# A small early read of w_in, one warm product fewer, and another order of the first layernorm tiles in a TensorE-bound kernel

## The chip, the cores and the metric

The kernel runs on one core of one Trainium2 chip. The metric is the device time of one execution in microseconds (us). Each kernel of a comparison is executed several times, in rounds that alternate with the kernel before on the same chip. A profile is a recording of one such execution; its span, from the first to the last instruction, is about 2.2 us shorter than the time.

## The reference, cut to what matters

x has 2048 rows of 640 numbers. The output is x plus two branches over xn = layernorm(x): a state-space branch and a gated MLP.

```python
xn = _layernorm(x, axis=-1)
return x + _A_ref(xn, ...) + _B_ref(xn, B_w_in, B_w_sp, B_b_sp, B_w_out)

def _B_ref(x, w_in, w_sp, b_sp, w_out):          # w_in: 640 x 1728
    z = _gelu(jnp.einsum('bsd,df->bsf', x, w_in))
    z1 = z[..., :Fh].copy()
    z2 = _layernorm(z[..., Fh:], axis=-1)
    g = jnp.einsum('ts,bsf->btf', w_sp, z2) + b_sp[None, :, None]   # 2048 x 2048
    return jnp.einsum('bsf,fd->bsd', z1 * g, w_out)
```

`_A_ref` (cut) is a complex diagonal recurrence over 2048 steps, with a dense product ahead of it and one behind it.

## The kernel before

The kernel records every operation with what it reads and writes, and then orders them itself: TensorE in program order, every other engine by priority. Constants such as `DMA_BW0` only steer this ordering; they change no hardware setting.

```python
class _Graph:
    EPS0 = 0.12
    DMA_BW = 280e3
    DMA_BW0, DMA_T0 = 225e3, 9.0
    ...
    # next operation of an engine: of those ready within EPS0, the one with the longest work behind it
    s0 = min(max(f, o.rdy) for o in lst)
    cand = max((o for o in lst if max(f, o.rdy) <= s0 + (self.EPS0 if s0 < self.TEPS else eps)), key=lambda o: o.tail)
```

x is worked on in 16 tiles of 128 rows, numbered from 0. In the head of the kernel, loads come from SyncE's queue in the order tile 0, 1, 2, two pieces of w_in, tile 3, a piece, tile 4, a piece, tile 5. TensorE first runs eight products of zeros ("warm").

```python
FIRST = "x0 x1 x2 h002 h025 x3 h103 x4 h135 x5"        # h..: pieces of w_in
...
NW = 8
for n in range(NW):
    pe(lambda e: e.matmul(ps[:, 7, :], zero_m.ap(128), zero_m.ap(512), start=True, stop=True), ..., 0.43, "warm")
```

Tiles 0 to 2 are handled early: only centred (`xc`, VectorE), transposed by TensorE (`T`), copied out of PSUM (`xnT`), multiplied with w_in in halves, and scaled by 1/std later, inside the GELU. The means of tiles 0 and 1 come from ScalarE (`lnmean`), the mean of tile 2 from statistics on VectorE (`bn2a`, `bn2b`, `bna2`). Tiles 3 and 6 get their sums from ScalarE (`lnsum`, `lnsq`, 0.72 us each) and then pass VectorE (`lnv`), GpSimd (`rstd`) and VectorE again (`xn`). Tile 4 gets statistics on VectorE (`bn4a`, `bn4b`). Its transposed copy `xnT4` is ScalarE's.

```python
dve(lambda e: e.tensor_scalar(xc.ap(D), xm.ap(D), mean, None, op0=ALU.subtract), [xm.iv(), mi], [xc.iv(0, 1280)], ..., "xc%d" % i)

def early_bn(i):
    x, xm = xs[i].ap(D), xs[i]
    held = [xc_m[2].iv()] if i == 1 else xnT_iv(2, 3) if i == 3 else []     # "held": also wait for these
    dve(lambda e: e.bn_stats(stv[:, i, 0:6], x[:, 0:320]), [xm.iv()] + held, [siv(i, 0, 6)], 0.41, "bn%da" % i)
    ...
pe(tr, [xn.iv(0, 1280), ident_m.iv()], [bank(b)] + ..., 0.3, "T%d" % i)
...
elif i in (1, 4, 6):
    act(lambda e: e.copy(xnTv[:, :, i * 128:(i + 1) * 128], v), [bank(b)], xnT_iv(i, i + 1), ca(D, psum=True), "xnT%d" % i)
```

The "first full tile" below is the first product of tile 4, the first that runs over all 864 columns in one go. From there on TensorE finds its work ready.

Much later, in the stage of w_sp ("spatial", a Strassen-like scheme of seven products for each of eight blocks), the gated results go through two buffers in turn, and a buffer is free again only when its store has landed:

```python
gm = g_m[ng[0] % 2]
...
dve(... e.tensor_tensor(gm.ap(FH), c.ap(FH), zm.ap(...), ALU.mult), ..., "gate%d%d" % (j, h))
...
dma("sp", g_d[n], gm.ap(896), [gm.iv()], [("gd", n, n + 1)], 128 * 1792, "gst%d%d" % (j, h), sem="gst%d" % gsem)
```

## Time and profile before

| | before |
|---|---|
| time, median of three runs | 262.68 us (262.36 to 262.86) |
| the profiled execution | 263.17 us, span 261.0 us |
| first full tile's products begin | 15.62 us |
| spatial stage begins / out stage begins / last product ends | 110.68 / 192.63 / 258.39 us |

First, lines of the profile's page: the span, the busy times of the engines (PE is TensorE, PEld its weight loads, DVE VectorE, ACT ScalarE, POOL GpSimd), and the shares of the chain of waits that ended last.

```profile
span 261.0 us, 4323 instructions
...
PE 256.0 (98%) x1501; PEld 152.0 (58%) x1501; DVE 243.9 (93%) x565; ACT 179.8 (69%) x323; POOL 26.9 (10%) x50
...
PE 95%; DMA 2%; ACT 1%; SPq 0%; issue 0%; DVE 0%
```

TensorE is busy 98% of the span and is 95% of the chain. So time can be won only where TensorE waits. The view of who waited for whom lists those places (engine, line, what it waited for: us in total, times, longest us):

```profile
PE ps L490 <- DVE arena L477: 1.2, 1, 1.2
PE ps L649 <- ACT arena L620: 0.7, 1, 0.7
PE ps L611 <- DVE arena L536: 0.3, 1, 0.3
PE ps L670 <- DMA arena<-in_B_w_in_dram: 0.2, 1, 0.2
```

All four lie in the head. The timeline of the head shows them in order (start, us, engine, line, operation, tiles, count, and in brackets the idle time just before with what ended it):

```profile
4.57 0.74 PE L611 MATMUL ps<-arena 128*128 128x128 bf16 x5
...
4.78 0.49 DVE L542 BATCH_NORM_STATS2 arena<-arena 128x6 f32<-128x320 bf16 x1 [0.43 <-DMA arena<-in_A_x_dram]
5.20 0.37 DVE L536 TENSOR_SCALAR arena<-arena 128x640 bf16<-128x640 bf16 x1
...
5.62 0.45 PE L611 MATMUL ps<-arena 128*128 128x128 bf16 x5 [0.31 <-DVE arena L536]
...
6.32 1.07 PE L670 MATMUL ps<-arena 128*128 128x432 bf16 x4 [0.25 <-DMA arena<-in_B_w_in_dram]
...
7.51 4.18 PE L670 MATMUL ps<-arena 128*128 128x432 bf16 x22
...
9.78 0.22 DVE L577 SCALAR_TENSOR_TENSOR arena<-arena 128x1 f32<-128x1 f32 x1 [1.46 <-ACT arena L575]
...
11.53 0.44 PE L611 MATMUL ps<-arena 128*128 128x128 bf16 x5
...
11.73 0.62 ACT L680 ACTIVATE arena<-ps,arena 128x432 bf16<-128x432 f32 x1 [0.78 <-PE ps L670]
...
12.34 0.72 ACT L573 ACTIVATE arena<-arena 128x640 bf16<-128x640 bf16 x1
...
13.61 0.44 PE L611 MATMUL ps<-arena 128*128 128x128 bf16 x5
...
13.66 0.73 ACT L575 ACTIVATE arena<-arena 128x640 bf16<-128x640 bf16 x1
...
14.88 0.69 ACT L620 COPY arena<-ps 128x640 bf16<-128x640 bf16 x1
...
15.62 0.91 PE L649 MATMUL ps<-arena 128*128 128x432 bf16 x4 [0.66 <-ACT arena L620]
```

Tile 1's centring (5.20) ran behind the statistics of tile 2 (4.78), which waited for tile 2's load, and tile 1's transposes (5.62) waited for it. And ScalarE idled 0.78 us before 11.73, then did the two sums of tile 6 (12.34 and 13.66) between GELUs, and so started the copy of tile 4 only at 14.88, 0.83 us after the transposes that it copies had ended (13.61 plus 0.44). TensorE waited 0.66 us for that copy.

### The profile page before, as it was taken

The page shows a single profiled execution, that of the slowest core. Times are in us where ns is not written, and L with a number is a line of the kernel's source. Part 1 is how long each engine was busy: PE and PEld are TensorE (multiplying, and loading weights), DVE is VectorE, ACT ScalarE, POOL GpSimd, SP SyncE. Part 2 cuts the span into 40 slices and gives each one's busy share as a digit, 9 for nine tenths or more (in the row PEclk, how much of TensorE's full clock was granted, in tenths as well). Part 3 has the DMA queues.
Part 4 walks back from the last instruction along what each step waited for, and adds up shares of the span by engine and source line. Part 5 has one row for each costly group of instructions (what it writes and reads, how often), then busy time and mean ns, then how long its engine had stood idle before and what let it go on. Part 6 is the DMA issues. An engine that isn't in the chain of part 4 may idle for free.

```text
span 261.0 us, 4323 instructions
## 1 busy us (share of the span) xinstructions
PE 256.0 (98%) x1501; PEld 152.0 (58%) x1501; DVE 243.9 (93%) x565; ACT 179.8 (69%) x323; POOL 26.9 (10%) x50
## 2 busy tenths in 40 slices
PE   7989999999999999999999999999999999999996
PEld 3555554444446777755555555555566677777774
DVE  5799999699999999999999999999999999999943
ACT  6799999989986445442333496865979897893110
POOL 3557265500000000000000000000000000000000
PEclk9999999999999999999999999999999999999999
DMA  6955689998505873399999966992133555545621
GB/s 188 332 107 103 136 176 211 241 301 219 81 0 125 166 201 136 104 313 192 230 222 187 244 156 136 232 242 69 54 113 95 139 146 121 148 134 157 171 104 53
DMA packets 89603, 42.31 MB, mean 162 GB/s; under 512 B 72334, under 2 KB 89582, under 8 KB 89582
## 3 DMA queue, kind: packets, MB, share of 16 engines
q1 hardware_dynamic: 89294, 41.93, 66.1%
q8 instruction: 12, 0.20, 0.3%
q10 hardware_dynamic: 288, 0.11, 0.2%
q14 instruction: 9, 0.07, 0.1%
HBM read 12.27 MB, written 12.45 MB: 95 GB/s over the span
## 4 chain that ended last, share of the span: by engine, by line
PE 95%; DMA 2%; ACT 1%; SPq 0%; issue 0%; DVE 0%
PE ps L1063 31%; PE ps L1211 23%; PE ps L649 20%; PE ps L743 17%; PE ps L670 2%; PE ps L1218 2%; DMA arena<-in_B_w_in_dram 2%; ACT arena L680 1%; SPq L373 0%; PE ps L611 0%; ACT arena L575 0%; ACT arena L573 0%; ACT arena L620 0%; DVE arena L1276 0%; PE ps L860 0%
## 5 line engine op out<-in xcount | busy, mean ns | idle before, releaser
L1063 PE MATMUL ps<-arena 128*128 128x432 bf16 x448 | 82.1, 346 | 0.0
L1063 PEld LDWEIGHTS ps<-arena 128*128 128x128 bf16 x448 | 43.6, 98 | 38.3 <-ACT arena L1076 0.9
L1211 PE MATMUL ps<-arena 128*128 128x320 bf16 (+2 forms) x456 | 64.7, 296 | 0.0
L1211 PEld LDWEIGHTS ps<-arena 128*128 128x128 bf16 x456 | 44.0, 98 | 17.3 <-ACT ps L1240 0.3
L649 PE MATMUL ps<-arena 128*128 128x432 bf16 x280 | 51.8, 346 | 0.7 <-ACT arena L620 0.7
L849 ACT ACTIVATE arena<-arena 128x512 bf16<-128x512 bf16 x70 | 46.3, 712 | 8.5 <-DVE arena L853 8.1
L649 PEld LDWEIGHTS ps<-arena 128*128 128x128 bf16 x280 | 34.6, 124 | 17.0 <-ACT arena L620 1.1
L743 PE MATMUL ps<-arena 128*128 128x512 bf16 x200 | 43.3, 379 | 0.0
L1076 ACT ACTIVATE arena<-ps,arena 128x432 f32<-128x432 f32 (+1 forms) x32 | 19.6, 617 | 22.7 <-PE ps L1063 22.7
L743 PEld LDWEIGHTS ps<-arena 128*128 128x128 bf16 x200 | 19.6, 98 | 23.5
L772 DVE SCALAR_TENSOR_TENSOR arena<-arena 128x512 f32<-128x512 bf16 x35 | 25.5, 742 | 0.0
L748 ACT CAST arena<-ps 128x512 bf16<-128x512 f32 x40 | 22.2, 600 | 3.6 <-PE ps L743 3.5
L853 DVE TENSOR_TENSOR arena<-arena 128x1024 bf16<-128x1024 bf16 (+1 forms) x42 | 23.9, 592 | 0.0
L727 ACT ACTIVATE arena<-ps 128x864 bf16<-128x864 f32 x16 | 14.2, 891 | 14.1 <-PE ps L649 11.6
L1232 DVE TENSOR_TENSOR arena<-ps,arena 128x320 bf16<-128x320 f32 (+1 forms) x40 | 18.6, 480 | 5.2 <-PE ps L1218 3.9
L1018 DVE TENSOR_TENSOR arena<-arena 128x1024 bf16<-128x1024 bf16 x32 | 21.0, 682 | 0.8 <-DMA arena<-in_B_w_sp_dram 0.8
L1240 ACT COPY ps<-ps 128x320 f32<-128x320 f32 x24 | 9.9, 413 | 16.5 <-PE ps L1211 16.3
L794 DVE TENSOR_TENSOR arena<-arena 128x512 f32<-128x512 f32 (+2 forms) x40 | 21.2, 548 | 0.0
L777 DVE SCALAR_TENSOR_TENSOR arena<-arena 128x256 bf16<-128x256 bf16 (+1 forms) x35 | 16.5, 475 | 0.0
L774 DVE SCALAR_TENSOR_TENSOR arena<-arena 128x256 bf16<-128x256 bf16 (+1 forms) x35 | 16.5, 473 | 0.0
L1178 DVE TENSOR_TENSOR arena<-arena 128x640 bf16<-128x640 bf16 x32 | 15.2, 479 | 0.0
L663 ACT ACTIVATE arena<-arena 128x864 bf16<-128x864 bf16 x12 | 11.2, 930 | 0.0
(116 smaller groups left out, 256.7 us busy)
## 6 DMA issues: line engine op xcount, KB each, us to landing
g_scratch<-arena SPq DMA_DIRECT2D x16, 224.0 KB, 2.8
z_scratch<-arena SPq DMA_DIRECT2D x16, 216.0 KB, 1.9
arena<-z_scratch SPq DMA_DIRECT2D x8, 432.0 KB, 4.4
arena<-in_A_x_dram SPq DMA_DIRECT2D x16, 160.0 KB, 3.3
base_scratch<-arena SPq DMA_DIRECT2D x16, 160.0 KB, 2.3
arena<-base_scratch SPq DMA_DIRECT2D x16, 160.0 KB, 2.3
out_dram<-arena SPq DMA_DIRECT2D x15, 160.0 KB, 2.3
arena<-in_B_w_in_dram SPq DMA_DIRECT2D x7, 216.0 KB, 4.4
```

What stands on the lines that cost most here:

```text
L649: r = e.matmul(ps[:, b + h, 0:FG], lhs(k), winv[:, k, hcol * FH + h * FG:hcol * FH + (h + 1) * FG], start=(k == 0), stop=(k == ND - 1))
L743: r = e.matmul(ps[:, b, :], btv[:, ri, k, q * 128:(q + 1) * 128], xnTv[:, k, tq * 512:(tq + 1) * 512], start=(k == 0), stop=(k == ND - 1))
L748: act(lambda e: e.copy(o[:, ri, tq], ps[:, b, :].rearrange("p (m j) -> p j m", j=8)), [bank(b)], [l_m.iv((q * 8 + j) * 1024 + ri * 512 + t ...
L772: dve(lambda e: e.scalar_tensor_tensor(tv, prev, lr, cur, op0=ALU.mult, op1=ALU.add), pr + [l_iv(q, j)] + cr, [t.iv()], cd(512) + PTR, nm ...
L794: tt = lambda o, a, b, op: (lambda e: e.tensor_tensor(o, a, b, op))
L849: act(lambda e, pv=pv, hv=hv, lo=lo, sc=sc: e.activation(pv, hv[:, lo:lo + 2, 1:257], ACT.Identity, scale=sc), [h.iv(), Civ(cn)], [m.iv((q ...
L853: dve(lambda e, mv=mv, lq=lq: e.tensor_tensor(lq, lq, mv, ALU.add), li + [m.iv(0, 1024 * n)], li, cd(512 * n, 2), "fix%s%d%d" % (nm, q0, j))
L1018: dve(lambda e: e.tensor_tensor(o.ap(1024), x.ap(1024), y.ap(1024), op), [x.iv(), y.iv()], [o.iv()], cd(1024, 2), "%s_%d" % (name, j))
L1063: r = e.matmul(ps[:, bk, 0:FG], lv_[:, k, :], rv[k], start=(first and k == 0), stop=(k == 7), skip_group_check=True)
L1076: act(lambda e: e.activation(o, pb(bk), ACT.Identity, bias=bias), [bank(bk)] + bi, [dst], ca(FG, psum=True, ptr=1), name)
L1211: r = e.matmul(ps[:, bk, c0:c1], lf(q), rf(q)[:, c0:c1], start=(first and q == 0), stop=(q == 7), skip_group_check=True)
L1232: dve(lambda e: e.tensor_tensor(o[0][:, c0:c1], ps[:, bk, c0:c1], y[0][:, c0:c1], ALU.add), [bank(bk), y[1]], [o[1]], cd(c1 - c0), "%s_%d" ...
```

## The change

The intent: let a tiny read (sixteen rows of w_in, 4 KB) make the first contact with w_in early from ScalarE's queue ("touch"); start the first transposes earlier by dropping a warm product; centre tile 1 before tile 2's statistics; and give the ordering model other figures, so that ScalarE and VectorE take their work in another order.

```diff
     DMA_BW = 280e3
+    DMA_BW1, DMA_T1 = 320e3, 14.0
     DMA_BW_T = 215e3
-    DMA_BW0, DMA_T0 = 225e3, 9.0
+    DMA_BW0, DMA_T0 = 205e3, 4.6
 ...
-                    dma_free = at + op.nbytes / (self.DMA_BW0 if at < self.DMA_T0 else self.DMA_BW)
+                    dma_free = at + op.nbytes / (self.DMA_BW0 if at < self.DMA_T0 else self.DMA_BW1 if at < self.DMA_T1 else self.DMA_BW)
 ...
+        dma("act", dk_m.ap(128)[0:16, :], B_w_in[0:640:40, FH:FH + 128], [], [dk_m.iv()], 4096, "touch", bias=9500)
 ...
-        NW = 8
+        NW = 7
 ...
-            held = [xc_m[2].iv()] if i == 1 else xnT_iv(2, 3) if i == 3 else []
+            held = [xc_m[2].iv()] if i == 1 else [xc_m[1].iv(0, 1280)] if i == 2 else xnT_iv(2, 3) if i == 3 else []
 ...
-            pe(tr, [...], [...], 0.3, "T%d" % i)
+            pe(tr, [...], [...], 0.5 if i == 0 else 0.3, "T%d" % i)
```

What it does to the built order of the head (g0.1 is the GELU of half 1 of tile 0). SyncE's order is unchanged.

```
ScalarE before: g0.0 lnsq3 g1.0 g2.0 g0.1 lnsum6 g2.1 lnsq6 g3.0 xnT4 g3.1 g1.1
ScalarE after:  g0.0 lnsq3 g2.0 g1.0 lnsum6 lnsq6 g0.1 g2.1 g1.1 xnT4 g3.0 g3.1
VectorE before: bna0 bn2a xc1 bn2b xnT0b bna2 xc2 bn1a bn1b xnT2 bna1 lnv3 bn4a bn4b bna4 xn3 ...
VectorE after:  bna0 xc1 bn2a bn2b xnT0b bna2 xc2 bn1a xnT2 bn1b bna1 bn4a bn4b lnv3 bna4 bn5a bn5b xn3 ...
```

More of the change, by code (lines that the diff above doesn't have):

```diff
@@ L612, in tr @@
                 return r
-            pe(tr, [xn.iv(0, 1280), ident_m.iv()], [bank(b)] + ([bank(6)] if i == 0 else []), 0.3, "T%d" % i)
+            pe(tr, [xn.iv(0, 1280), ident_m.iv()], [bank(b)] + ([bank(6)] if i == 0 else []), 0.5 if i == 0 else 0.3, "T%d" % i)
             if i == 0:
```

## The prediction

Its "third transposes" are those of tile 3, its "fifth tile" is tile 4.

> **What bounds the kernel now.** TensorE. The page has PE busy 98% of a 261.0 us span, and the chain of waits is 95% PE. From 18.2 us on, the timeline shows its products back to back. The view of who waited for whom gives PE four waits: 1.2 us at the start, 0.3 us for the centred second tile (VectorE), 0.2 us for the first w_in piece (DMA), 0.7 us for ScalarE's copy of the transposed fifth tile. So only the head, up to the first full tile's products at 15.62 us, can change and its gain should reach the end, since later work moves along with it.
>
> **What the change does, by timeline and build order**. PE: one warm product fewer. ScalarE: one DMA issue first; the two sums over tile 6 now stand ahead of the last three half-tile GELUs, where they stood among them. VectorE: second tile centred before the third's statistics; fifth tile's statistics ahead of a wait on ScalarE. SyncE: unchanged.
>
> **Costs.**
> 1. Warm product: the first transposes were ready at 4.24 us (centring ends) but queued behind the eighth warm product (4.15, spaced 0.43 us) and began at 4.57. With seven they begin at about 4.3: -0.28 us.
> 2. Centring of tile 1: its mean is there at 4.54, but VectorE waited for the third tile (landed 4.76) and did its statistics first, centring at 5.20. Now about 4.56: -0.64. Its transposes' copy ends near 6.45 instead of 6.81.
> 3. Touch: the first w_in piece landed at 6.28, but 15 of its 16 parts were in by 5.45; one packet took 1.3 us. If first contact with w_in is the cause, the touch hides it: piece 1 at 5.5 to 5.9, later loads 0 to 0.4 us earlier. The Trainium skill (DMA: Bandwidth & Descriptors, Issuing engines are not separate DMA queues) says both queues share the same 16 engines; no run here shows that yet. On ScalarE the issue costs about 0.45 us (SyncE's issue spacing), table load 1.28 us, then a 0.2 us activation: done near 2.7, before tile 0 lands at 2.96. Free.
> 4. Together the 22-product block starts near 7.15 instead of 7.51. Without faster loads this is lost again at the third transposes (11.53), which hang on tile 3's landing (7.58) through ScalarE and GpSimd.
> 5. ScalarE idled 10.95 to 11.73, then did two tile sums (0.72 each), so the fifth tile's copy came at 14.88 although its transposes were done at 14.07. Now the first sum fills that hole: copy at about 14.03, done 14.7. PE's 0.66 us stall before 15.62 nearly vanishes: first full tile near 14.75 (14.4 with faster loads).
>
> **Predicted.** 0.85 us (loads unchanged) to 1.2 us off; taken as 1.0 off. 261.7 us, 8 in 10 between 261.1 and 262.4; faster by over 2% 0.005, within 2% 0.985, slower 0.01.
>
> **What would show it.** First transposes at 4.3; second copy ending 6.45; first w_in product before 6.0; tile 4's copy near 14.0; first full tile at 14.4 to 14.8; later stages unchanged.
>
> **What would make it wrong.** The touch's slow first reads delaying tile 0 itself (it gates the whole head); the slow packets being random, not first contact; ScalarE late for tile 0; the PE clock rising later: warm products run every 0.43 us against 0.216 later, and the Trainium skill (TensorE: Matmul & The Clock Gate, The HAM clock gate) says a free-running window of about 3.4 us decides that, so it may differ from run to run.

## The result, and the profile after

| | before | after |
|---|---|---|
| median of six runs, same chip | 262.72 us (262.17 to 262.86) | 262.49 us (261.87 to 263.36) |
| mean of six runs | 262.61 | 262.51 |
| ratio, with 95% interval | | 0.9996 (0.9976 to 1.0017) |
| span of the profiled execution | 261.0 | 260.6 |
| first full tile | 15.62 | 14.95 (-0.67) |
| spatial stage begins | 110.68 | 110.00 (-0.68) |
| out stage begins | 192.63 | 192.14 (-0.49) |
| last product ends | 258.39 | 257.90 (-0.49) |

A ratio is the mean time of one kernel's fast runs over that of the other's of the same rounds, so it is not quite the ratio of the medians, or of the means of all runs. The time is the same within the interval: 0.1 us off in the mean, where 1.0 was predicted, and the median lies 0.1 us above the top of the predicted range. The interval reaches from about 0.6 us faster to 0.4 us slower, so this measurement alone rules out 1.0 but not a gain of half a microsecond.

The page, as before (span, TensorE, chain):

```profile
span 260.6 us, 4320 instructions
...
PE 256.2 (98%) x1496; PEld 152.0 (58%) x1500; DVE 244.3 (94%) x565; ACT 180.2 (69%) x323; POOL 26.4 (10%) x50
...
PE 92%; DMA 3%; DVE 1%; SPq 1%; issue 1%; ACT 0%; POOL 0%
```

TensorE's waits:

```profile
PE ps L494 <- DVE arena L481: 1.2, 1, 1.2
PE ps L1067 <- ACT arena L1080: 0.2, 1, 0.2
```

Three of the four waits are gone from the list, as intended. A new one of 0.2 us has come up in the spatial stage (L1067 is its products, L1080 its evictions on ScalarE). It is 0.36 us of idle TensorE at 180.4 when the neighbouring products are counted, and it is where the lead of 0.68 us becomes 0.49.

The timeline of the head, to be set against the one of before:

```profile
4.39 1.43 PE L615 MATMUL ps<-arena 128*128 128x128 bf16 x10
...
4.67 0.39 DVE L540 TENSOR_SCALAR arena<-arena 128x640 bf16<-128x640 bf16 x1 [0.21 <-ACT arena L535]
...
5.77 1.52 PE L674 MATMUL ps<-arena 128*128 128x432 bf16 x4
...
7.41 4.18 PE L674 MATMUL ps<-arena 128*128 128x432 bf16 x22
...
9.19 0.49 DVE L587 BATCH_NORM_STATS2 arena<-arena 128x6 f32<-128x320 bf16 x1 [0.44 <-DMA arena<-in_A_x_dram]
...
9.99 0.20 DVE L581 SCALAR_TENSOR_TENSOR arena<-arena 128x1 f32<-128x1 f32 x1
...
10.82 0.73 ACT L577 ACTIVATE arena<-arena 128x640 bf16<-128x640 bf16 x1
...
11.68 0.74 ACT L579 ACTIVATE arena<-arena 128x640 bf16<-128x640 bf16 x1
...
11.69 0.45 PE L615 MATMUL ps<-arena 128*128 128x128 bf16 x5
...
13.66 0.44 PE L615 MATMUL ps<-arena 128*128 128x128 bf16 x5
...
14.20 0.69 ACT L624 COPY arena<-ps 128x640 bf16<-128x640 bf16 x1
...
14.95 0.90 PE L653 MATMUL ps<-arena 128*128 128x432 bf16 x4
```

Tile 1 is centred at 4.67 and its transposes follow tile 0's without a gap (ten in one row at 4.39). The first w_in product runs at 5.77 instead of 6.32; the trace has the first piece of w_in landing at 5.50 instead of 6.28. The block of 22 products, however, starts only 0.10 us earlier (7.41), because the four products ahead of it, which began early, ran at the slow clock: 1.52 us where they had taken 1.07. Tile 3's transposes begin at 11.69, later than before, although tile 3 landed earlier (7.09 against 7.58). VectorE took tile 4's statistics first (9.19, which waited 0.44 us for tile 4's load), and `lnv3`, whose inputs were ready at 9.6, came behind them at 9.99; in before it ran at 9.78, ahead of tile 4's statistics. Then the part that worked: the two sums of tile 6 now stand at 10.82 and 11.68, the first in ScalarE's old hole, and the copy of tile 4 starts at 14.20, 0.10 us after its transposes ended (they began at 13.66).

So in these two profiles the whole gain of the head is the order on ScalarE. That leaves four questions. Is it the ScalarE order in general? Is the touch worth anything? Is what was gained in the head given back in the spatial stage? And why do the times show less than the profiles?

### The profile page after: what moved, and what is told of

Same layout as the page of the kernel before. It is cut to its first block, busy times and chain, and to the rows that moved or that the text cites. A ratio compares the mean times of both kernels' runs of the same rounds, so it can differ in the third digit from the quotient of the medians.

```text
span 260.6 us, 4320 instructions
## 1 busy us (share of the span) xinstructions
PE 256.2 (98%) x1496; PEld 152.0 (58%) x1500; DVE 244.3 (94%) x565; ACT 180.2 (69%) x323; POOL 26.4 (10%) x50
## 4 chain that ended last, share of the span: by engine, by line
PE 92%; DMA 3%; DVE 1%; SPq 1%; issue 1%; ACT 0%; POOL 0%
PE ps L1067 29%; PE ps L1215 23%; PE ps L653 20%; PE ps L747 16%; DMA arena<-in_A_x_dram 2%; PE ps L1222 2%; DMA arena<-in_B_w_sp_dram 1%; SPq L374 1%; PE ps L674 1%; PE ps L615 0%; DVE arena L1022 0%; ACT arena L853 0%; DVE arena L857 0%; POOL arena L594 0%; ACT arena L1080 0%
## 5 line engine op out<-in xcount | busy, mean ns | idle before, releaser
L1067 PE MATMUL ps<-arena 128*128 128x432 bf16 x448 | 82.1, 346 | 0.2 <-ACT arena L1080 0.2
L1067 PEld LDWEIGHTS ps<-arena 128*128 128x128 bf16 x448 | 43.7, 98 | 38.4 <-ACT arena L1080 0.9
L1080 ACT ACTIVATE arena<-ps,arena 128x432 f32<-128x432 f32 (+1 forms) x32 | 19.7, 617 | 22.8 <-PE ps L1067 22.8
L747 PEld LDWEIGHTS ps<-arena 128*128 128x128 bf16 x200 | 19.6, 98 | 23.5
L731 ACT ACTIVATE arena<-ps 128x864 bf16<-128x864 f32 x16 | 14.2, 891 | 14.0 <-PE ps L653 11.1
L667 ACT ACTIVATE arena<-arena 128x864 bf16<-128x864 bf16 x12 | 11.1, 928 | 0.0
```

The costliest lines, as they stand in the source:

```text
L747: r = e.matmul(ps[:, b, :], btv[:, ri, k, q * 128:(q + 1) * 128], xnTv[:, k, tq * 512:(tq + 1) * 512], start=(k == 0), stop=(k == ND - 1))
L1067: r = e.matmul(ps[:, bk, 0:FG], lv_[:, k, :], rv[k], start=(first and k == 0), stop=(k == 7), skip_group_check=True)
L1080: act(lambda e: e.activation(o, pb(bk), ACT.Identity, bias=bias), [bank(bk)] + bi, [dst], ca(FG, psum=True, ptr=1), name)
```

## The experiments

In most experiments the order of each engine is written out as a list and enforced, since otherwise every edit would move other instructions as well. "Gap" below is the time from tile 3's transposes to the first full tile, the stretch that ScalarE's order decides. Each profile is one execution; where a statement rests on several, it says on how many. All outputs were correct. Each experiment is compared with eleven runs of the kernel before on the same chip.

### First call: one part of the change alone, or all but one

**act_only**: the kernel before with ScalarE's order of the change, nothing else.

```diff
-  g0.0 lnsq3 g1.0 g2.0 g0.1 lnsum6 g2.1 lnsq6 g3.0 xnT4 g3.1 g1.1
+  g0.0 lnsq3 g2.0 g1.0 lnsum6 lnsq6 g0.1 g2.1 g1.1 xnT4 g3.0 g3.1
```

> The kernel before with one thing changed: ScalarE's order of the changed kernel (both sums over tile 6 ahead of the last three half-tile GELUs of tiles 0 to 2, the fifth tile's copy ahead of tile 3's GELUs). No touch, eight warm products, VectorE order of before. Theory A (the order on ScalarE is all of the gain in the head; touch, warm product and centring give nothing that lasts): first full tile's products at 14.9 to 15.0 us instead of 15.62, third transposes still near 11.5, time 0.4 to 0.7 us below the kernel before. Theory B (the touch and the earlier centring carry the gain): full tile no earlier than 15.3, time within 0.3 us of before.

Measured: ratio 0.9982 (0.9959 to 1.0006), median 262.75 against 263.41 us. Its timeline:

```profile
12.08 0.45 PE L642 MATMUL ps<-arena 128*128 128x128 bf16 x5
...
14.80 0.69 ACT L651 COPY arena<-ps 128x640 bf16<-128x640 bf16 x1
...
15.55 0.91 PE L680 MATMUL ps<-arena 128*128 128x432 bf16 x4
```

The copy of tile 4 starts at 14.80, 0.17 us after its transposes ended, and the gap is 3.47 us where the kernel before had 4.09. The profiled head as a whole was not ahead of the first profile of before (15.55 against 15.62), because tile 3 landed late in this execution (8.16), which put its transposes at 12.08. The same execution waited 0.6 us for the transposing load of tile 8 near 22.6 us. What follows: the order on ScalarE alone takes 0.6 us off the gap. The start of the tile and the time, which theory A put at 14.9 to 15.0 us and 0.4 to 0.7 us below before, are less clear: 15.55, and 0.40 us in the mean.

**touch_only**: the kernel before with the touch, nothing else.

```diff
+        dma("act", dk_m.ap(128)[0:16, :], B_w_in[0:640:40, FH:FH + 128], [], [dk_m.iv()], 4096, "touch", bias=9500)
```

> The kernel before plus the touch alone. Theory A (slow DMA packets are scattered, not a first contact with w_in): about 20 packets of w_in over 150 ns as in both traces so far, first piece of w_in landing anywhere from 5.4 to 6.3, time within 0.2 us of before. Theory B (first contact): first piece at 5.5 or earlier, no w_in packet over 500 ns, and the loads behind it earlier; even so at most 0.2 us faster, since ScalarE still holds the full tile at 15.6.

Measured: ratio 1.0008 (0.9986 to 1.0029), median 263.68. The first piece of w_in landed at 5.64, tile 3 at 7.10, and tile 2 at 5.07, later than before's 4.76. In its timeline tile 1's transposes then wait for tile 2's statistics, just as the order of before makes them:

```profile
5.09 0.49 DVE L575 BATCH_NORM_STATS2 arena<-arena 128x6 f32<-128x320 bf16 x1 [0.66 <-DMA arena<-in_A_x_dram]
...
5.93 0.71 PE L644 MATMUL ps<-arena 128*128 128x128 bf16 x5 [0.62 <-DVE arena L569]
```

Tile 3's transposes came at 12.10, the full tile at 16.19, the gap was 4.09 again. The touch alone gives no time.

**no_touch**: the change without the touch (its other orders kept).

```diff
-        dma("act", dk_m.ap(128)[0:16, :], B_w_in[0:640:40, FH:FH + 128], [], [dk_m.iv()], 4096, "touch", bias=9500)
```

> The changed kernel without the touch, every order as in the changed kernel. Theory A: the same as the changed kernel within 0.2 us (mean near 262.5), full tile near 14.9. Theory B: 0.4 us or more slower than the changed kernel, first w_in piece landing near 6.2 again. A third possibility, that the touch itself costs: tile 0 lands at 2.96 instead of 3.06 and this is 0.1 us faster.

Measured: ratio 0.996 (0.9938 to 0.9982), median 262.42. The full tile was at 14.91, with w_in landing at 6.03. So the head of the change is had without the touch.

**after_fixed**: the change itself, orders written out: a repetition on this chip.

> The changed kernel again, built with its orders written out (same instructions), as a repeat and a check of the writing-out. Expected as the changed kernel: 262.1 to 262.7 median, ratio 0.998 to 1.000, full tile at 14.8 to 15.2, third transposes at 11.5 to 11.8. If the changed kernel's 0.67 us in the head is real in every run, the ratio over five rounds should be near 0.9975; if it is lost again in the spatial stage, the start of that stage is 0.6 us early and the last product less than 0.3 us early.

Measured: ratio 0.9971 (0.9948 to 0.9994), median 262.72, full tile 15.22. Here the change is 0.69 us faster in the mean (262.65 against 263.34). In the first measurement it was 0.10. The change's own level hardly moved (262.51 there, 262.65 here); that of the kernel before did (262.61 there, 263.34 here).

The spans say the same more clearly. Mean span of the runs: before 261.16, act_only 260.78, touch_only 261.43, no_touch 260.20, after_fixed 260.22.

No_touch and after_fixed both waited in the spatial stage near 168 us. In no_touch the waits of VectorE and of TensorE there, from the view of who waited for whom:

```profile
DVE arena L1135 <- DMA g_scratch<-arena: 1.0, 1, 1.0
```

```profile
PE ps L1094 <- ACT arena L1107: 0.6, 1, 0.6
```

and the timeline of that stretch:

```profile
164.62 0.61 DVE L1135 TENSOR_TENSOR arena<-arena 128x864 bf16<-128x864 bf16 x1 [1.03 <-DMA g_scratch<-arena]
...
165.74 1.34 ACT L880 ACTIVATE arena<-arena 128x512 bf16<-128x512 bf16 x2 [1.03 <-DVE arena L845]
...
166.98 0.60 ACT L1107 ACTIVATE arena<-ps,arena 128x432 f32<-128x432 f32 x1
...
167.63 1.27 PE L1094 MATMUL ps<-arena 128*128 128x432 bf16 x6 [0.56 <-ACT arena L1107]
```

This is a chain. A gate product on VectorE (L1135) waits 1.03 us for a store out of the buffer that it is to write; the trace has that store issued at 159.51 and landed at 164.60, 5.1 us later, where the median of such stores is 2.8. (In before it took 4.5 us, 160.23 to 164.71.) VectorE's next results (L845) come late, so ScalarE's rotation (L880) waits 1.03 us, so the eviction of a spatial product (L1107) starts only at 166.98, so TensorE waits 0.56 us for the bank. The theory now had a rival to test: that a faster head only arrives earlier at this wait and gives its lead back there.

### Second call: take the wait for the store away

**after_g3**, **before_g3**: the change and the kernel before with a third gate buffer. **best_g3**: the third buffer, no touch, and `lnv3` ahead of tile 4's statistics, `xnT4` ahead of g1.1.

```diff
+        g_m.append(Mem(st_m.lo, 1792))           # space that is free by then
-                gm = g_m[ng[0] % 2]
+                gm = g_m[ng[0] % 3]
-            gsem = n % 2
+            gsem = n % 3
```

> The changed kernel with a third buffer for the gated tile (the statistics' memory, free by then), so that gate product 40 on VectorE need not wait for the store of gate 30. Theory A (the head's gain is taken back near 167.7 us, where TensorE waits for ScalarE, which waits for VectorE, which waits for that store): no TensorE wait over 0.1 us near 167 to 169, from the spatial stage's first product to the last product of all 147.7 to 148.0 us instead of 148.2 to 148.65, time 0.3 to 0.5 us below the changed kernel, ratio to before 0.995 to 0.9965. Theory D (VectorE is late there by its own work, or any transfer in that congested stretch would do): a wait of 0.3 us or more stays within 160 to 185 us and the interval stays above 148.2.

> The kernel before with the third gate buffer, nothing else. Theory A: TensorE waited only 0.12 us there in the profile of before, so at most 0.2 us faster than before (ratio 0.999 to 1.000), interval from first spatial product to the last 147.8 to 148.0. If the store also held the kernel before in most of its runs, up to 0.4 us faster.

> Changed kernel without the touch, third gate buffer, and two moves in the order: on VectorE tile 3's variance step ahead of tile 4's statistics (so that it doesn't wait for tile 4's landing), on ScalarE the fifth tile's copy ahead of tile 1's second GELU. Theory A (the VectorE order of the change holds the third transposes behind tile 4's landing): third transposes at 11.1 to 11.3 instead of 11.55 to 11.76, first full tile at 14.4 to 14.6 instead of 14.9 to 15.2, time 0.7 to 1.0 us below the changed kernel, ratio to before 0.992 to 0.9945. If tile 4's landing isn't what holds it: third transposes stay at 11.5 or later and the gain is the buffer's alone.

Measured: after_g3 1.0014 (0.9994 to 1.0035), before_g3 1.0035 (1.0011 to 1.0059), best_g3 1.0042 (1.0014 to 1.007). All three are above 1, and the wait was still there. Best_g3 missed in the head as well. With `lnv3` ahead of tile 4's statistics tile 3's transposes were expected at 11.1 to 11.3 and came at 11.72, because `xn3` still stood behind tile 5's statistics (11.22). In best_g3:

```profile
DVE arena L1185 <- DMA g_scratch<-arena: 2.3, 1, 2.3
```

```profile
PE ps L1144 <- ACT arena L1157: 1.7, 1, 1.7
```

The edit was wrong. It hands out buffers in program order, but VectorE runs the gates of the later blocks in swapped pairs (gate 41 before gate 40), so the third buffer moved the wait for the same store to a gate that runs even earlier. The runs that were to remove the wait made it longer. They still serve, as the far end of a scale (VectorE's wait for the store, and TensorE's wait behind it, in the same profile; from the same view for every profile):

| VectorE waited | TensorE waited | in |
|---|---|---|
| 2.3 | 1.7 | best_g3 |
| 1.5 | 0.9 | before_g3 |
| 0.9 to 1.0 | 0.2 to 0.7 | act_only, no_touch, after_fixed, dve_only2, after_g3, and from the fifth call warm_only |
| up to 0.6 | none | before, touch_only, and from later calls head2, after_rep, no_touch_rep, after_w8 |
| none | none | after_g3x, head2_g3x, after_g3x_rep, no_touch_g3x (below) |

The first profile of after belongs in the fourth row too (0.3, none near 168); its 0.2 us wait lies at another place. The view leaves out short waits: in after_w8 it lists none of TensorE's, yet that spatial stage took 82.52 us where after_rep's took 81.79.

Does a faster head run into this wait more? The kept traces can say. In all twelve profiles with two buffers that store is issued 49.55 us after the spatial stage begins, whatever the head did, so the lead is not spent before it. What differs is how long the store takes. In the seven profiles where it took 4.5 to 5.1 us the stage took 81.95 to 82.74 us; in the five where it took 4.1 to 4.4 us the stage took 81.8 us in four, and 82.14 in after, which lost its time at 180.4. The store took 4.59 us in the mean of the three such profiles with both orders of before, and 4.57 in the six with both orders of the change; the stage took 82.17 and 82.19 us. So no more is lost there behind a faster head.

**dve_only2**: the kernel before with the change's orders on VectorE and GpSimd, nothing else.

```diff
-  bna0 bn2a xc1 bn2b xnT0b bna2 xc2 bn1a bn1b xnT2 bna1 lnv3 bn4a bn4b bna4 xn3 ...
+  bna0 xc1 bn2a bn2b xnT0b bna2 xc2 bn1a xnT2 bn1b bna1 bn4a bn4b lnv3 bna4 bn5a bn5b xn3 ...
```

> The kernel before with the VectorE (and GpSimd) order of the changed kernel alone: second tile centred first; no touch, eight warm products, ScalarE order of before. Theory A: second tile's transposes at 5.05 to 5.2 whatever the third tile's landing (5.57 to 5.93 with the order of before), third transposes at 11.5 to 11.8 (11.5 to 12.1 with the order of before), but the full tile still 4.0 us after the third transposes, so 15.6 to 15.8: time within 0.3 us of before. Theory B (the centring carries the gain): 0.5 us or more faster.

Measured: ratio 1.0016 (0.9996 to 1.0035), median 263.67. Tile 1's transposes followed tile 0's without a gap, as intended. Tile 3's came at 12.08 (tile 3 landed at 8.16 in this execution) and the full tile at 15.88. So the centring is moved as wanted, and the time doesn't follow: the head hangs on later loads. The gap was 3.80, so this order too takes 0.29 us off it when it stands alone.

The parts do not add up in time. Against before: ScalarE order -0.40 us, touch +0.27, VectorE order +0.38, which makes +0.25, while the whole change in the same session gave -0.69. Each of these has an error of a few tenths, and each carries the luck of its loads; the parts on their own are too small for this.

### Third call: the third buffer in running order, and a better order of the head

**before_g3x**, **after_g3x**: buffers handed out in the order in which VectorE runs the gates.

```diff
+        GB = [0] * 16
+        for n, w in enumerate((0, 1, 2, 3, 4, 5, 7, 6, 9, 8, 11, 10, 13, 12, 14, 15)):
+            GB[w] = n % 3
-                gm = g_m[ng[0] % 3]
+                gm = g_m[GB[2 * j + h]]
```

> The first third-buffer kernels handed the buffers out in program order, which put the wait for the store of gate 30 on gate product 41, earlier still, and lost 1 us there. Here the three buffers go round in the order in which the products run, so that no gate product waits for a store less than 4 us old. Kernel before otherwise. Theory A: no TensorE wait near 168, interval from first spatial to last product 147.7 to 148.0, time 0 to 0.3 us below before (ratio 0.9985 to 1.000). Theory D: the wait near 168 stays.

> Changed kernel with the three buffers in running order. Theory A: the lead in the head now reaches the end: no TensorE wait over 0.1 us near 168, interval 147.7 to 148.0 (148.2 to 148.65 in the changed order with two buffers), ratio to before 0.994 to 0.996. Theory D: interval stays at 148.2 or more and ratio at 0.997.

Measured: before_g3x 0.998 (0.9948 to 1.0011), after_g3x 0.9974 (0.9943 to 1.0004). The profile of before_g3x fell in a slow execution (301 us) and is not used; its five other runs are. In after_g3x neither VectorE nor TensorE waits in the spatial stage. The third buffer takes the kernel before from 263.53 to 262.92 us in the mean, within the noise (the interval holds 1). That the wait for the store can cost time is shown by the scale above and by its absence here. That it takes the change's lead back in particular is not what the store's times above show; warm_only, with all orders of before, meets the wait as well.

**head2**: the change with `lnv3` ahead of tile 4's statistics, `xn3` ahead of tile 5's, `xnT4` ahead of g1.1. **head2_g3x**: the same with the third buffer.

```diff
-  ... bna1 bn4a bn4b lnv3 bna4 bn5a bn5b xn3 bna5 bn7a xnT3 ...      (VectorE)
+  ... bna1 lnv3 bn4a bn4b bna4 xn3 bn5a bn5b bna5 bn7a xnT3 ...
-  ... g2.1 g1.1 xnT4 ...                                             (ScalarE)
+  ... g2.1 xnT4 g1.1 ...
```

> Changed kernel, two buffers as in it, but a faster head: on VectorE tile 3's variance step ahead of tile 4's statistics and its normalisation ahead of tile 5's; on ScalarE the fifth tile's copy ahead of tile 1's second GELU. Theory A: third transposes at 10.9 to 11.3, first full tile at 14.2 to 14.6, 0.5 us ahead of the changed kernel, yet the last product no more than 0.2 us ahead of it, with a TensorE wait of 0.8 to 1.3 us near 168: ratio to before near 0.997, as the changed kernel. Rival (a lead in the head reaches the end): ratio 0.995.

> The faster head and the three buffers together, touch kept. Theory A: both gains show: full tile at 14.2 to 14.6, interval 147.7 to 148.0, ratio to before 0.992 to 0.995, the fastest of all. If another transfer takes the store's place as the limit near 160 to 185 us, the wait moves there and the ratio stays at 0.996 or above.

Measured: head2 0.9996 (0.9964 to 1.0028), head2_g3x 0.9988 (0.9953 to 1.0023). In head2:

```profile
11.20 0.44 PE L692 MATMUL ps<-arena 128*128 128x128 bf16 x5
...
12.90 1.09 PE L751 MATMUL ps<-arena 128*128 128x432 bf16 x5 [0.53 <-DVE arena L704]
...
13.82 0.44 PE L692 MATMUL ps<-arena 128*128 128x128 bf16 x5
```

Tile 3's transposes came at 11.20, before the 11.69 of the first profile of the change. That `lnv3` behind tile 4's statistics held them there is read from that profile; head2 does not show it, since with the change's own order they came at 10.99 in another execution (after_rep, below). And now tile 5's statistics stand between `xn3` and the copy `xnT3`; TensorE waited 0.53 us for that copy before 12.90, tile 4's transposes came 2.6 us after tile 3's instead of 2.0, and the full tile was at 15.05. Nothing was gained: the work moved out of the way of one step stands in the way of the next. Head2_g3x had the full tile at 15.35. Both missed the 14.2 to 14.6 and the ratios expected.

### Fourth call: repetitions on another chip

**after_rep** is the change, **no_touch_rep** is no_touch, **after_g3x_rep** is after_g3x, and **no_touch_g3x** is after_g3x without the touch.

```diff
-        dma("act", dk_m.ap(128)[0:16, :], B_w_in[0:640:40, FH:FH + 128], [], [dk_m.iv()], 4096, "touch", bias=9500)
```

> The changed kernel itself, word for word, on one chip with the three below. So far its ratio was 0.9996 on one chip and 0.9971 on another. Theory A: 0.997 to 0.999, with a TensorE wait of 0.3 to 0.8 us near 168 or 180 in the profile; full tile at 14.8 to 15.2. If the first measurement was the typical one: 0.9990 or more.

> The changed kernel without the touch again. Theory A: within 0.3 us of after_rep, either sign. Theory B (touch brings the first loads forward in the mean): first w_in piece and tile 3 land 0.3 us or more later than in after_rep, and it is 0.2 us or more slower in the mean of its fast runs.

> Changed kernel with three gate buffers in running order, again. Theory A: interval from first spatial to last product 147.7 to 148.0, 0.3 to 0.6 us below after_rep in the mean. If the store's wait is not what takes the lead: within 0.2 us of after_rep.

> Changed kernel without the touch, with three gate buffers. Theory A: as after_g3x_rep within 0.3 us, interval 147.7 to 148.0, both below the two kernels with two buffers.

| | ratio | tile 3's transposes | full tile |
|---|---|---|---|
| after_rep | 0.9976 (0.9954 to 0.9997) | 10.99 | 14.45 |
| no_touch_rep | 0.9989 (0.9967 to 1.0011) | 11.18 | 14.65 |
| after_g3x_rep | 0.9967 (0.9948 to 0.9987) | 11.76 | 15.23 |
| no_touch_g3x | 0.9974 (0.9954 to 0.9994) | 12.01 | 15.47 |

The change is faster by 0.68 us in the mean here (262.40 against 263.08), again at its usual level. Change minus no_touch, in the three pairs of the same call: +0.21, -0.35, -0.23 us. The second pair leans to the touch (first piece of w_in at 5.27 against 5.88, tile 3 at 7.06 against 7.26), the first pair against it. The touch is worth a few tenths at most, and even its sign is not settled. The third buffer took 0.23 us off after_rep and 0.34 off no_touch_rep in the mean, less than or at the low end of the 0.3 to 0.6 expected; and the wait expected in after_rep's spatial stage is not in its profile.

### Fifth call: the warm product

In the runs with seven warm products so far, the time was in about a third of them not 2.15 but 2.3 to 3.1 us longer than the span; in the kernels with eight it never was. So: **warm_only**, the kernel before with seven; **after_w8**, the change with eight.

```diff
-        NW = 8                        (warm_only; after_w8 has the opposite edit on the change)
+        NW = 7
```

> The kernel before with seven warm products instead of eight, nothing else. In every run so far of a kernel with eight warm products (30 runs of five kernels, and every listed run of before) the time reported is 2.0 to 2.25 us above the traced span; in a third of the runs of kernels with seven (24 of 72) it is 2.3 to 3.1. Theory E (the missing warm product itself brings this time outside the span): one or more of the six runs at 2.3 or above, span the same as before, time 0 to 0.3 us slower than before in the mean. Rival (the orders of ScalarE and VectorE together, or the earlier finish, bring it): all six at 2.0 to 2.25. First transposes at 4.2 to 4.4 instead of 4.57 either way, and nothing of it left at the full tile.

> The changed kernel with eight warm products as in before; touch and all orders as changed. Theory E: all six runs at 2.0 to 2.25 us above their span; first transposes at 4.57 again, full tile within 0.2 us of the changed kernel's 14.5 to 15.2, so 0 to 0.3 us faster than the changed kernel in the mean: ratio to before 0.996 to 0.998. Rival: two of six runs still at 2.3 or above.

Measured: warm_only 1.0009 (0.9975 to 1.0042), its six runs from 263.16 to 266.6 us, 0.75 us above before in the mean, 0.28 without the slowest. The slowest is the profiled one, and TensorE's timeline says why:

```profile
4.36 0.71 PE L690 MATMUL ps<-arena 128*128 128x128 bf16 x5
5.70 0.72 PE L690 MATMUL ps<-arena 128*128 128x128 bf16 x5 [0.62 <-DVE arena L615]
6.21 1.89 PE L749 MATMUL ps<-arena 128*128 128x432 bf16 x4
7.89 0.74 PE L690 MATMUL ps<-arena 128*128 128x128 bf16 x5
```

Three groups of five 128x128 transposes took 0.71 to 0.74 us, and these four products of 432 columns 1.89, where the warm clock gives 0.44 and (in before) 1.07. The record of the clock turned to full speed only at 10.56 us; in the profiles of before and after it did at 5.44 and 6.93. Tile 3's transposes came at 13.50 and the full tile at 17.59, 2 us late. This one execution does not tie the late clock to the dropped product: over the profiles that record the rise it came at 3.96 to 10.56 us with seven (nine profiles) and at 4.50 to 7.16 with eight (six), at 6.08 in the mean of either.

After_w8: 0.9972 (0.9947 to 0.9998), median 262.91, six runs within 262.45 to 263.09, the first transposes at 4.58 and the full tile at 14.87. The dropped warm product is not needed for the gain. Time above span: all six runs of after_w8 between 2.14 and 2.21 us, one of six of warm_only at 2.88. Together with all listed runs: above 2.3 us in 25 of 78 with seven warm products, in none of 35 with eight, and in none of 55 runs of the kernel before. It is no rule for each kernel (after_g3x_rep and no_touch_rep, with seven, had none in six runs each). What happens in that time the trace does not hold; only that it goes with having seven products is shown. For the change it is 0.10 to 0.25 us in the mean of six runs (mean excess over the span, less that of the kernel before).

## Why the prediction was right or wrong

**The change helps, but by less than 1.0 us in the time, and in the first measurement by almost nothing.** Over all profiles with both orders of before (three: before, touch_only, before_g3; the late clock of warm_only left out) tile 3's transposes come at 11.76 us and the full tile at 15.85. Over the ten with both orders of the change (after, no_touch, after_fixed, after_g3, after_g3x, after_rep, no_touch_rep, after_g3x_rep, no_touch_g3x, after_w8) they come at 11.47 and 14.91. That is 0.94 us in the head, of which 0.65 lies in the gap. The gap was 4.09 us in all four profiles with both orders of before, warm_only among them, 3.47 in act_only, 3.80 in dve_only2, and 3.3 to 3.5 in the ten: in the gap, ScalarE's order alone gives what the whole change gives. The other 0.29 us, tile 3's transposes, rests on touch_only (12.10; the other two give 11.60), where tile 2's late load and the late clock (7.16) held TensorE's block of 22 products. Elsewhere tile 3's own load all but decides: in 13 of the 19 profiles of fast runs the transposes begin 3.92 to 4.05 us after it has landed, whatever the order (in before, before_g3 and after_w8 the block of 22 ends a little later still), and that landing varied from 6.96 to 8.16. So the spread of the tile's start within one kind (14.45 to 15.47), as large as the effect, is in the main that of one load.

- **Bound and place** (TensorE, only the head can change): right. From the first full tile on, TensorE's work was the same, and the lead held to the spatial stage within 0.01 us.
- **Step 1, the warm product**: the start at 4.39 was near the 4.3 predicted. What it missed is the cost: time outside the span was added in a third of the runs. In the profile of after the clock also came later (6.93) and the early products ran slow, but that is luck, as the profiles with eight products show (4.50 to 7.16). The warning that the clock may differ from run to run was in the prediction; warm_only shows its worst case.
- **Step 2, the centring**: right in place (4.67 for 4.56; copy ended 6.55 for 6.45).
- **Step 3, the touch**: the first piece landed at 5.50, as predicted, and no load was earlier in a way that can be told from chance. First contact is not the cause of slow packets. Over all profiles, packets of w_in above 150 ns were 19.6 of 1280 with the touch (10 profiles) and 21.0 without (9), those above 500 ns 3.4 and 3.3. The first piece landed at 5.57 in the mean with the touch and 5.80 without, each spread over 0.7 us or more; tile 3 at 7.32 and 7.59. Tile 0 was not delayed (2.98 and 2.99). The Trainium skill (DMA: Bandwidth & Descriptors, Issuing engines are not separate DMA queues) says that transfers from either queue run on the same 16 engines and that a second issuer saves only issue time; no trace here shows on which engines the touch ran.
- **Step 4, the block of 22 products**: 7.41 for 7.15. The products ahead of it ran on the cold clock, which the sum had left out. That the lead would be lost again at tile 3's transposes was right in kind, but these hung in the profile of after on tile 4's load through VectorE's new order, which the prediction had noted ("fifth tile's statistics ahead of a wait on ScalarE") and not costed.
- **Step 5, the copy of tile 4**: right. 14.20 for 14.03, full tile 14.95 for 14.75. Act_only shows it alone.

**The step that failed is the sum: "taken as 1.0 off", on the ground that "its gain should reach the end".** The mechanism in the head held. The head gave 0.67 us and not 1.0, and of that 0.4 us reached the end of the profiled span and 0.10 the mean time; what the dropped warm product adds outside the span was left out. From 1.0 to the 0.10 us of the first measurement, in means (the terms are read from one pair of profiles and six runs each, so they are an account of this measurement and not sizes to expect again):

1. The head gave 0.67 in the two profiles, 0.33 short: 0.15 was an allowance for faster loads, which did not come (0.85 to 1.0), and tile 3's transposes came 0.16 later, not at the same time.
2. The spans differ by 0.4: another 0.27 was given back, of it 0.19 in the spatial stage, at the wait at 180.4, where before had none, and the rest after the last product. By the store's times above this is chance, not a bottleneck that follows a faster head: with two buffers, waits of 0.2 to 0.6 us in that stage appear in profiles with either orders (no_touch, after_fixed; warm_only) and are missing in others of each (after_rep, no_touch_rep; before, touch_only).
3. The profile of before was of an execution slower than all six timed ones. Before's six runs, less the 2.17 us that its profiled run had above its span, give an estimated mean span of 260.44; the six of after have 260.20. That leaves 0.24 and takes 0.16 off the 0.4.
4. Outside the span the change is 0.14 longer (0.45 us in two of its six runs), which leaves 0.10.

In two later calls, on two chips, the same kernels differ by 0.69 and 0.68 us in time and by 0.95 and 0.78 in mean span. There the prediction's -0.85 to -1.2 holds for the span, at its lower end or just below, and falls short in time by what lies outside the span. The change's level is steady (262.51, 262.65, 262.40); the kernel before had 262.61 in the first measurement and 263.08 to 263.53 in the five later sets. Why it was some 0.7 us better there is open: one profile of that session was to be had, and it was of a slower run.

That the time would stay within 2% was right; the range of 261.1 to 262.4 was too narrow. Its base was not the fault, 262.68 from three runs against 262.72 in the measurement; it left no room for a gain of less than 0.3 us.

No version beats the change beyond doubt. The change with eight warm products (0.9972) and with the third buffer in running order (0.9974 and 0.9967) are as fast, the first without the long runs.

## What to carry to other kernels

Look for an engine that idles before a batch of optional work and is late for the next copy that TensorE needs: moving the optional work into its own hole was the one part of this change that showed in every profile. When one operation is put ahead of another on an engine, ask what it waits for, since the one behind it waits for that too (`lnv3` behind a load that it did not need). And where the effect is below half a per cent, read stage positions over several profiles and take the base from several chips: one profile of a head that hangs on loads can be off by half a microsecond, and the three runs of before that agreed within 0.5 us lay, in the mean, 0.4 to 0.9 us below the five later sets.

## What the Trainium skill lacked or had wrong

- TensorE: Matmul & The Clock Gate (The HAM clock gate) gives a free-running window of 3413 ns, and start-to-start times of 426.7 and 215.7 ns for 512 columns when cold and warm. The trace agrees: warm products every 0.43 us, later products of that size every 0.216. The rise was recorded between 3.96 and 10.56 us in these profiles. The page doesn't say how full a window must be, and these profiles don't settle it: if the recorded rise marks the end of a window, TensorE was busy for 2.77 us of the one that raised the clock at 3.96 (best_g3), and also for 2.77 us of the one that ended 3.41 us before the rise at 10.56 and did not raise it (warm_only); both are estimates, from the page's window and the traces' times. The page's advice that the ramp is below 1% of a span is true here (the full tile of warm_only was 2 us late, of 264) and is still several times this change's effect.
- DMA: Bandwidth & Descriptors (Anatomy of one DMA) gives a fixed cost of about 2.0 us, for transfers issued by GpSimd. The first load, issued by SyncE, took 2.2 us from issue (0.74) to landing (2.96), with the moving of its 164 KB in it, which is near. No page tells of scattered slow packets: some 20 of 1280 packets of w_in took above 150 ns where the median took 40, and one of 1.3 us put a landing at 6.28 although 15 of its 16 parts were in by 5.45. The page's line of 0.2 us mean and 2 us at high load for memory access (Latency and other measured facts) spans them, without saying how often they come.
- No page says how much later than its like a single store can land among other transfers of its queue: 4.1 to 5.1 us in every profile of a fast run where the median of such stores was about 2.8, and up to 1.7 us of TensorE's time behind it (best_g3).
- No page speaks of time outside the span that differs between executions of one kernel: 2.0 to 2.25 us in all runs of kernels with eight warm products, 2.3 to 3.1 in 25 of 78 with seven. Its cause is open.
